# Out1's PSUM tiles regrouped from halves of the result to bank numbers, with other load times in the planner

## The chip, the cores and the metric

The kernel runs on one core of one Trainium2 chip. The time is device microseconds of one execution, compared as the median of several runs. TensorE (PE) has a queue of its own, as have VectorE (DVE), ScalarE (ACT), GpSimd (POOL) and SyncE (SP); each works off its queue in order, and engines wait for each other through semaphores. TensorE writes its results to PSUM (eight banks), and ScalarE and VectorE take them from there to SBUF.

## What is computed

The reference, cut to what matters (B = 8 batches, H = 8 heads, S = 576 tokens, D = 64, M = 32 memory slots; d_model 512, d_ff 2048):

```python
a = softmax(phi over S)                        # (B, H, S, M)
k_m, v_m = a^T k, a^T v                        # (B, H, M, D)
x = softmax(q k_m^T / 8) v_m                   # (B, H, S, D) -> (4608, 512)
h = x @ moe_w_in;  x = silu(h) @ moe_w_out     # first layer
h = x @ moe2_w_in; y = elu(h) @ moe2_w_out     # second layer
```

## The kernel before

**Arithmetic.** All is fp32. Large products are made of fp16 parts: an operand is split into a high and a low part, and a product is the sum of three matmuls (low x high, high x low, high x high; `mm3`). In the first layer the attention's output is not formed: `v_m` is multiplied into `w_in` first (`u_mm`, tile `u`), and the in1 product is attention weights `aT` times `u`.

**Stages.** A hand-written list does batch 0's attention and in1 and loads the first weights (to about 75 us). `plan_first` then plans the rest of batch 0's out1 and the batches 1 to 7: for each batch in1 (16 steps m, each 12 matmuls into one PSUM tile `ph`, followed by a silu on ScalarE) and out1 (below), beside which run the attention of a later batch (scores, softmax, transposes, `kvp`, `u`) and the conversion of the second layer's weights (`raw` to `quad` to `hl_q`, stored to `w2is` and `w2os` by POOL's queue). A second plan does the last batch's out1 and the whole second layer in nine token blocks (`h2A`, `h2D`, `o`).

**Out1 of a batch** (`plan_out1`) is a Strassen-like scheme: seven products j in the order 0, 1, 5, 6, 4, 3, 2 (p1, p2, p6, p7, p5, p4, p3 in the code). Each consists, for the two halves e = 0, 1 of the output features, of 8 units q; a unit is 3 matmuls of 128 x 288. The moving operands `T` are split from sums of `h` by ScalarE and VectorE. Products 0, 5, 4, 2 accumulate one after the other in bank 0, products 1, 6, 3 in bank 1 (`BANK`). After each product ScalarE copies (`copy_of`, line 177 `y<-ph`) or VectorE adds (`add_to`, line 1251 `y<-ph,io,y`) its bank to the result `y`, once for each half. POOL then stores a half of `y` to `x2d` (line 1280), and ScalarE squares it once that store has landed (line 353).

**PSUM.** Four banks are the pool `ps_m`, two tiles of two banks with one tag "m", handed out in turn. In in1 a tile holds one step m (two token halves). In out1 a tile holds one half e: its bank 0 and its bank 1.

**The planner** (`Plan`) takes tasks with an engine, a cost in us, a rank and dependences, simulates the engines, and emits the instructions in the simulated order. Products are main tasks with due times spread evenly over the plan; every other task is due ahead of what needs it by the costs between and, ahead of a product, by AHEAD. Weight conversions get due times between W2FROM and W2TO of the plan. Buffers are rings: a task that takes a slot depends on those that free it. Waits between engines are put in afterwards, from what instructions read and write; the planner's dependences are its own. A load costs 3.6 us + KB/350 in `plan_first` and depends on its ring's slot: `kv` has 3 slots and ten loads for each batch, q four.

Of the kernel before, what the change touches and what calls it, by code (L numbers as in the profile page):

```python
# [38 lines left out]
SA = 2.0 ** 14  # L39
NY = 2  # L40
NT = 3
NKV = 3
W2FROM, W2TO, AHEAD = 0.2, 0.92, 25
SHIFT = 9
WB_TAG = ("w0", "w1", "w2", "T2")
WR = ("w0", "w2", "w1")
# [43 lines left out]
def attn_moe_moe(ctx: ExitStack, tc: tile.TileContext, qT, phiT, kvm, kvt, w1i, w1o, w2i, w2o, out):  # L90
# [8 lines left out]
    dram = ctx.enter_context(tc.tile_pool(name="dram", bufs=1, space=bass.MemoryType.DRAM))  # L99
    ps_a = ctx.enter_context(tc.tile_pool(name="ps_a", bufs=4, space=PSUM))  # L100
    psum = ctx.enter_context(ExitStack())
    ps_m = psum.enter_context(tc.tile_pool(name="ps_m", bufs=2, space=PSUM))

    x2d = [dram.tile([P, KD, S], F32, name=f"x2d{b}") for b in range(B)]

# [81 lines left out]
    class Plan:  # L187
# [41 lines left out]
                        latest[d] = min(latest[d], latest[i] - self.tasks[d][1] - wait - (self.ahead if i in main else 0.0))  # L229
            self.tasks = [(t[0], t[1], latest[i], *t[3:]) for i, t in enumerate(self.tasks)]  # L230

        def load(self, kb, rank, fn, deps=()):

            return self.add("DMA", (2.2 if self.ahead is None else 3.6) + kb / 350, rank, fn, deps, kb / 350)

        def store(self, kb, rank, fn, deps=()):

# [646 lines left out]
    def plan_mem(pl, n, r, ex, ready):  # L884
# [21 lines left out]
        for g in range(NG):  # L906
            for c in range(NC):
                load, free = [], []
                if n > 1:
                    load = [pl.load(256, r - 300, lambda g=g, c=c: load_kv(n, g, c), pl.ring("kv", NKV))]  # L910
                    free = pl.take("kv", load[0])
                elif c == NC - 1:
                    free = pl.rings["kv"][1 + g][1]
                t = on("PE", 0.3, lambda g=g, c=c: mem_kv(n, g, c), load + es + (last or pl.ring(*C)))
                if not last:
                    kv_free = pl.take("c", t)
                last = [t]
                free.append(t)
            kv += last
# [43 lines left out]
    def plan_attn(pl, n, r, mem, after):  # L963


        A = "a", 2

        def on(eng, cost, fn, deps):
            return pl.add(eng, cost, r, fn, deps)

        qs, q_frees = [], []
        for p in range(NP):
            if n > 1:
                qs.append(pl.load(295, r - 290, lambda p=p: load_q(n, p), pl.ring("q", NP)))
# [55 lines left out]

    HALF = [slice(0, HS), slice(HS, S)]

    def ps_half():
        ps = ps_m.tile([P, 2, 512], F32, tag="m", name="ph")
        return ps[:, :, :HS], [ps[:, 0, :HS], ps[:, 1, :HS]]

    def y_tile(name="y"):
# [5 lines left out]

    def in1_first(m):
        z = st[0]
        pv, ps = ps_half()
# [6 lines left out]
    def plan_out1_first(pl, rank, ready):  # L1053
# [5 lines left out]

        def mm(d, q):  # L1060
            if q == 0:
                z[d] = ps_half()
            ks = range(4 * q, 4 * q + 4)
            for k in ks:
                for t in range(2):
# [6 lines left out]
        for d in range(KD):  # L1072
            for q in range(4):
                t = pl.product(4.25, rank + 4 * d + q, lambda d=d, q=q: mm(d, q),
                           last + ready[d] + (pl.ring("m", 2) if q == 0 else []))
                if q == 0:
                    free = pl.take("m", t)
# [9 lines left out]
    def plan_in1(pl, b, r, A, u, u_free, first, h_free):  # L1087
# [2 lines left out]
        z = st[b]  # L1090
        w = {}
        silus = []

        def mm(m):
            w[m], ps = ps_half()
            mm3(ps, HALF, [
                (z["u", g][:, 0, m * P:(m + 1) * P], z["u", g][:, 1, m * P:(m + 1) * P], z["aT"][:, 0, g], z["aT"][:, 1, g])
                for g in range(NG)
# [4 lines left out]
                out=h[m // KQ][:, :, m % KQ], in_=w.pop(m), func=AF.Silu, scale=z["inv1"][:, m // 4:m // 4 + 1])  # L1103

        for m in range(KF):
            t = pl.product(1.475, r + m, lambda m=m: mm(m), A["aT"] + [u[m // 4, g] for g in range(NG)] + pl.ring("m", 2))
            for free in u_free + [A["aT_free"]]:
                free.append(t)
            free = pl.take("m", t)
# [70 lines left out]
    def plan_out1(pl, b, r, silus, made, stored, scales, y_tile, y_ring):  # L1180

        z = st[b]
        w = [dict() for _ in range(2)]
        BANK = {0: (0, 0), 5: (0, 8), 4: (0, 16), 2: (0, 24), 1: (1, 0), 6: (1, 0), 3: (1, 8)}
        io = pl.add("DVE", 0.25, r - 2500, lambda: out_scale(b), scales + list(stored.values()))
        loads = {}

# [6 lines left out]

        def unit(e, j, q):
            bank, at = BANK[j]
            if "ps" not in w[e]:  # L1200
                w[e]["ps"] = ps_half()[1]
            t = z["T", WSEQ.index(j)]
            mm3([w[e]["ps"][bank]], [slice(0, HS)], [
                (w1s[b, j][:, e, 0, q], w1s[b, j][:, e, 1, q], t[:, 0, q], t[:, 1, q])
            ], at + q, at + KQ, skip_group_check=at > 0)

        last = {}
        free = {}
        took = {}
        count = [0]  # L1210

        def units(j, e, q, deps):
            bank = BANK[j][0]
            if e not in free:
                deps = deps + pl.ring("m", 2)
            t = pl.product(0.368, r + 0.5 * count[0], lambda: unit(e, j, q),
                       deps + [last.get((e, bank)), took.get(e), loads[j][0]] + z["made"].get((MOVING[j], q // 4), []))
            count[0] += 1
            if e not in free:
                free[e] = pl.take("m", t)  # L1220
                took[e] = t
            last[e, bank] = t
            loads[j][1].append(t)
            z["T_free", WSEQ.index(j)].append(t)
            return t

        def product(j, deps):

            t = [None, None]
            load(j)  # L1230
            if WSEQ.index(j) >= made:
                plan_moving(pl, b, WSEQ.index(j), r - 2400, silus)
            if j in (3, 2):
                for e in range(2):
                    for q in range(KQ):
                        t[e] = units(j, e, q, deps[e])
            else:
                for q in range(KQ):
                    for e in range(2):
                        t[e] = units(j, e, q, deps[e])  # L1240
            return t

        def copy_of(e, bank, s, deps):
            def fn():
                if "y" not in w[e]:
                    w[e]["y"] = y_tile()
                acopy(w[e]["y"][:, s], w[e]["ps"][bank], z["io1"][:, e:e + 1])
            return pl.add("ACT", act(HS), r - 2500, fn, deps)

        def add_to(e, bank, s, from_, deps):  # L1250
            return pl.add("DVE", dve(HS), r - 2500, lambda: nc.vector.scalar_tensor_tensor(
                out=w[e]["y"][:, s], in0=w[e]["ps"][bank], scalar=z["io1"][:, e:e + 1], in1=w[e]["y"][:, from_],
                op0=ALU.mult, op1=ALU.add), deps)

        E = range(2)
        C11, C12, C21, C22 = range(4)
        p1 = product(0, [[], []])
        yfree = []
        c1 = []
        for e in E:  # L1260
            c1.append(copy_of(e, 0, C11, [p1[e], io] + pl.ring(*y_ring)))
            yfree.append(pl.take(y_ring[0], c1[e]))
        p2 = product(1, [[], []])
        c11 = [add_to(e, 1, C11, C11, [c1[e], p2[e]]) for e in E]
        p6 = product(5, [[c] for c in c1])
        u2 = [copy_of(e, 0, C21, [p6[e], c1[e]]) for e in E]
        p7 = product(6, [[c] for c in c11])
        s7 = [copy_of(e, 1, C22, [p7[e], c1[e]]) for e in E]
        p5 = product(4, [[c] for c in u2])
        c22 = [add_to(e, 0, C22, C22, [p5[e], s7[e]]) for e in E]  # L1270
# [585 lines left out]
```

## Time and profile before

| | |
|---|---|
| median of 3 runs | 1422.68 us (1421.36 to 1424.61) |
| profiled execution, its own time | 1424.17 us |
| its span (first to last instruction) | 1422.4 us |
| busy: TensorE, VectorE, ScalarE, POOL | 1357.5, 1127.4, 952.3, 51.3 us |
| mean granted TensorE clock | 0.991 of full |

The span is what one profiled execution took from its first to its last instruction; the 1.8 us beside it lie around that. Busy time is the union of an engine's instructions. Idle time of an engine that is not the bottleneck costs nothing by itself. The ends of matmuls are modelled, and consecutive matmuls overlap in the listing. Line numbers are those of the code above; many matmuls have line 1019, that of the helper `mm3`, so they are told apart by their tiles: `ph<-aT,u` is in1, `ph<-T,w1s` out1.

### The profile page before, as it was taken

Reading aid. Unit: us, or ns where it says so; the run is one execution under the profiler, and the core shown is the slowest. Engines: PE = TensorE matmul, PEld = TensorE weight load, DVE = VectorE, ACT = ScalarE, POOL = GpSimd, SP = SyncE. Lnnn points to the kernel's source line nnn. Section 1 sums busy time; section 2 is a strip of 40 time slices with the busy share of each in tenths; the row PEclk is TensorE's granted clock in tenths of the full one; section 3 lists DMA queues with packets and bytes.
Section 4 is the critical chain, followed back from the end, with each engine's and each line's share of the span. In section 5 each row is a group of like instructions: output and inputs, shape, how many; then the busy total and the mean of one; then the engine's idle time right before and its main releaser. Section 6 shows DMA issues by size and latency. Waiting matters only on the chain.

```text
span 1422.4 us, 28662 instructions
## 1 busy us (share of the span) xinstructions
PE 1357.5 (95%) x12048; PEld 1092.2 (77%) x12048; DVE 1127.4 (79%) x1753; ACT 952.3 (67%) x1357; POOL 51.3 (4%) x85
## 2 busy tenths in 40 slices
PE   4998999999998999999998999999999999999998
PEld 3676667676766767676777888888888888888887
DVE  5878878788877988796767788787978787878794
ACT  3667765858756686675657576767767676857582
POOL 0001100010110010001000000000000000000000
PEclk8999999999999999999999999999999999999999
DMA  9465767467466475645195333242415151414130
GB/s 362 169 212 176 259 250 265 154 234 262 174 239 232 169 275 185 226 151 198 53 345 175 106 108 109 85 131 68 149 41 175 41 167 49 148 63 137 59 119 31
DMA packets 68801, 233.07 MB, mean 164 GB/s; under 512 B 9024, under 2 KB 15168, under 8 KB 64064
## 3 DMA queue, kind: packets, MB, share of 16 engines
q1 hardware_dynamic: 60288, 199.78, 41.6%
q0 software_dynamic: 8384, 31.46, 5.6%
q8 instruction: 94, 1.54, 0.5%
q14 instruction: 35, 0.29, 0.1%
HBM read 186.12 MB, written 40.89 MB: 160 GB/s over the span
## 4 chain that ended last, share of the span: by engine, by line
PE 73%; DMA 8%; DVE 7%; ACT 7%; issue 4%; SPq 0%; POOL 0%; ACTq 0%; POOLq 0%; DVEq 0%
PE ph L1019 24%; PE o L1019 20%; PE h2A L1019 11%; PE h2D L1019 8%; DMA wi<-w2is 3%; PE ph L1066 2%; PE up L859 2%; PE sc L774 2%; DMA kv<-in_kvm 2%; PE kvp L678 1%; PE ph L1026 1%; DMA w2is<-hl_q 1%; DVE h L133 1%; DMA raw<-in_w1o 1%; ACT y L177 1%
## 5 line engine op out<-in xcount | busy, mean ns | idle before, releaser
L1019 PE MATMUL o<-t,wq 128*128 128x256 f16 x3024 | 361.1, 273 | 1.8 <-DVE t L174 1.5
L1019 PEld LDWEIGHTS <-wi 128*128 128x128 f16 x3024 | 295.7, 98 | 49.2 <-issue 7.2
L1019 PEld LDWEIGHTS <-wq 128*128 128x128 f16 x3024 | 295.8, 98 | 37.0 <-issue 2.3
L1019 PE MATMUL ph<-T,w1s 128*128 128x288 f16 x2352 | 307.3, 286 | 12.3 <-ACT y L177 7.4
L1019 PEld LDWEIGHTS <-w1s 128*128 128x128 f16 x2352 | 226.2, 98 | 82.4 <-issue 26.2
L1019 PE MATMUL h2A<-xh,wi 128*128 128x256 f16 x1728 | 227.8, 273 | 9.3 <-ACT h L1460 5.2
L1460 ACT ACTIVATE h<-h2A,inv 128x256 f32<-128x256 f32 x288 | 133.2, 468 | 115.4 <-PE h2A L1019 112.1
L1019 PE MATMUL ph<-aT,u 128*128 128x288 f16 x1344 | 176.3, 286 | 1.3 <-ACT h L1102 1.0
L1019 PE MATMUL h2D<-xh,wi 128*128 128x256 f16 x1296 | 171.0, 274 | 0.1
L169 ACT ACTIVATE t<-h,s_g 128x768 f16<-128x768 f32 (+1 forms) x144 | 147.0, 1036 | 33.7 <-DVE h L1502 23.0
L174 DVE SCALAR_TENSOR_TENSOR t<-h,s_g,t 128x768 f16<-128x768 f32 (+1 forms) x144 | 162.9, 1144 | 5.7 <-ACT t L169 5.6
L1019 PEld LDWEIGHTS <-u 128*128 128x128 f16 x1344 | 127.0, 98 | 49.2 <-issue 18.9
L174 DVE SCALAR_TENSOR_TENSOR T<-h,c,T 128x1152 f16<-128x1152 f32 x98 | 137.0, 1411 | 19.5 <-ACT T L169 19.4
L1464 DVE SCALAR_TENSOR_TENSOR h<-h2D,inv,h 128x256 f32<-128x256 f32 x216 | 102.1, 479 | 60.7 <-PE h2D L1019 46.6
L169 ACT ACTIVATE T<-h,c 128x1152 f16<-128x1152 f32 x98 | 119.9, 1250 | 33.0 <-DVE h L133 22.2
L133 DVE TENSOR_TENSOR h<-h 128x256 f32<-128x256 f32 (+1 forms) x302 | 128.3, 462 | 3.0
L1502 DVE SCALAR_TENSOR_TENSOR h<-e,h 128x1024 f32<-128x1024 f32 x72 | 87.9, 1221 | 18.6 <-ACT e L1498 18.0
L1102 ACT ACTIVATE h<-ph,inv 128x576 f32<-128x576 f32 x112 | 81.7, 738 | 15.9 <-PE ph L1019 15.3
L1495 ACT ACTIVATE e<-h 128x1024 f32<-128x1024 f32 x72 | 75.5, 1049 | 14.1 <-DVE h L1464 13.8
L1498 ACT ACTIVATE e<-e 128x1024 f32<-128x1024 f32 x72 | 75.7, 1051 | 0.9
L1066 PE MATMUL ph<-h,w1o 128*128 128x288 f32 x256 | 66.1, 415 | 0.0
L133 DVE TENSOR_TENSOR h<-h,h 128x1152 f32<-128x1152 f32 x42 | 56.5, 1352 | 8.2 <-ACT h L1102 7.8
(183 smaller groups left out, 1279.2 us busy)
## 6 DMA issues: line engine op xcount, KB each, us to landing
w1s<-w1os SPq DMA_DIRECT2D x98, 512.0 KB, 4.6
wi<-w2is SPq DMA_DIRECT2D x56, 896.0 KB, 4.6
kv<-in_kvm SPq DMA_DIRECT2D x48, 256.0 KB, 5.1
q<-in_qT SPq DMA_DIRECT2D x32, 288.0 KB, 7.3
out<-ye SPq DMA_DIRECT2D x36, 256.0 KB, 2.0
raw<-in_w1i SPq DMA_DIRECT2D x8, 1024.0 KB, 11.3
raw<-in_w1o SPq DMA_DIRECT2D x8, 1024.0 KB, 4.9
raw<-in_w2i SPq DMA_DIRECT2D x8, 1024.0 KB, 6.9
```

The lines of the kernel that those rows point to most:

```text
L133: nc.vector.tensor_tensor(out=out, in0=a, in1=b, op=op)
L169: nc.scalar.activation(out=hi, in_=x, func=AF.Copy, scale=s)
L174: nc.vector.scalar_tensor_tensor(out=lo, in0=x, scalar=s, in1=hi, op0=ALU.mult, op1=ALU.subtract)
L774: nc.tensor.matmul(ps[o:o + 64, c // 2, 2 * p:2 * p + 2], z["q", p][:, t0:t0 + 64], z["kT"][:, p // 2, 64 * (p % 2):64 * (p % 2) + 64], st ...
L1019: nc.tensor.matmul(o, w, x[:, c], start=first, stop=last, **how)
L1066: nc.tensor.matmul(z[d][1][t], wB[d][:, k], h[k // KQ][:, t, k % KQ], start=(k == 0), stop=(k == KF - 1))
L1102: nc.scalar.activation(out=h[m // KQ][:, :, m % KQ], in_=w.pop(m), func=AF.Silu, scale=z["inv1"][:, m // 4:m // 4 + 1])
L1460: nc.scalar.activation(out=w["x"][:, s], in_=w["A"], func=AF.Copy, scale=inv)
L1464: return pl.add("DVE", COST["add"], base, lambda: nc.vector.scalar_tensor_tensor(out=w["x"][:, s], in0=w["D"], scalar=inv, in1=w["x"][:, s ...
L1495: nc.scalar.activation(out=w["e"], in_=w["x"][:, B21:], func=AF.Relu, scale=-1.0)
L1498: nc.scalar.activation(out=w["e"], in_=w["e"], func=AF.Exp, scale=-1.0)
L1502: nc.vector.scalar_tensor_tensor(out=x, in0=w["e"], scalar=-1.0, in1=x, op0=ALU.add, op1=ALU.max)
```

## The change

Out1's two PSUM tiles are taken by bank number: one tile holds bank 0 of both halves, the other bank 1 of both halves. The pool has two tags m0 and m1 with one tile each; in1's steps alternate between them, `mslot` keeps which is next. Units of all seven products now alternate between the halves, and every dependence on a product is one on both halves' last units. The copies that follow p3 free the one tile, the additions that follow p4 the other. In the planner, loads of `kv` are costed 1 us later (the 64-row tail 3 us, and at 128 KB), those of q 3 us later; W2TO goes from 0.92 to 0.95 and AHEAD from 25 to 35.

```diff
+KVLATE, QLATE = 1.0, 3.0
-W2FROM, W2TO, AHEAD = 0.2, 0.92, 25
+W2FROM, W2TO, AHEAD = 0.2, 0.95, 35
-    ps_m = psum.enter_context(tc.tile_pool(name="ps_m", bufs=2, space=PSUM))
+    ps_m = psum.enter_context(tc.tile_pool(name="ps_m", bufs=1, space=PSUM))
-        def load(self, kb, rank, fn, deps=()):
-            return self.add("DMA", (2.2 if self.ahead is None else 3.6) + kb / 350, rank, fn, deps, kb / 350)
+        def load(self, kb, rank, fn, deps=(), late=0.0):
+            return self.add("DMA", (2.2 if self.ahead is None else 3.6) + late + kb / 350, rank, fn, deps, kb / 350)
-                    load = [pl.load(256, r - 300, lambda g=g, c=c: load_kv(n, g, c), pl.ring("kv", NKV))]
+                    load = [pl.load(256 if c < NC - 1 else 128, r - 300, lambda g=g, c=c: load_kv(n, g, c), pl.ring("kv", NKV), KVLATE if c < NC - 1 else 3.0)]
-                qs.append(pl.load(295, r - 290, lambda p=p: load_q(n, p), pl.ring("q", NP)))
+                qs.append(pl.load(295, r - 290, lambda p=p: load_q(n, p), pl.ring("q", NP), QLATE))
-    def ps_half():
-        ps = ps_m.tile([P, 2, 512], F32, tag="m", name="ph")
+    mslot = [0]
+    def ps_half(k):
+        ps = ps_m.tile([P, 2, 512], F32, tag=f"m{k}", name="ph")
# plan_in1 (in1_first and plan_out1_first likewise)
+        at = mslot[0]
-            w[m], ps = ps_half()
+            w[m], ps = ps_half((at + m) % 2)
-            t = pl.product(1.475, r + m, lambda m=m: mm(m), A["aT"] + [u[m // 4, g] for g in range(NG)] + pl.ring("m", 2))
+            t = pl.product(1.475, r + m, lambda m=m: mm(m), A["aT"] + [u[m // 4, g] for g in range(NG)] + pl.ring(f"m{(at + m) % 2}", 1))
# plan_out1
+        SLOT = mslot[0], 1 - mslot[0]
+        mslot[0] = SLOT[1]
         def unit(e, j, q):
             bank, at = BANK[j]
-            if "ps" not in w[e]:
-                w[e]["ps"] = ps_half()[1]
+            if bank not in ps:
+                ps[bank] = ps_half(SLOT[bank])[1]
-            mm3([w[e]["ps"][bank]], [slice(0, HS)], [
+            mm3([ps[bank][e]], [slice(0, HS)], [
         def units(j, e, q, deps):
-            if e not in free:
-                deps = deps + pl.ring("m", 2)
+            if bank not in free:
+                deps = deps + pl.ring(f"m{SLOT[bank]}", 1)
         def product(j, deps):
-            if j in (3, 2):
-                for e in range(2):
-                    for q in range(KQ):
-                        t[e] = units(j, e, q, deps[e])
-            else:
-                for q in range(KQ):
-                    for e in range(2):
-                        t[e] = units(j, e, q, deps[e])
-            return t
+            return [units(j, e, q, deps) for q in range(KQ) for e in range(2)][-2:]
-        p6 = product(5, [[c] for c in c1])
-        u2 = [copy_of(e, 0, C21, [p6[e], c1[e]]) for e in E]
+        p6 = product(5, c1)
+        u2 = [copy_of(e, 0, C21, [c1[e]] + p6) for e in E]
...
-        c22 = [add_to(e, 0, C22, C22, [p5[e], s7[e]]) for e in E]
+        c22 = [add_to(e, 0, C22, C22, [s7[e]] + p5) for e in E]
-        p3 = product(2, [[c] for c in c22])
+        p3 = product(2, c22)
+        free[0] += c12
+        free[1] += c21
-            free[e] += [c11[e], c21[e], c12[e], c22[e]]
```

## Rows read from the trace of the kernel before

**Rows 1.** Summary: busy time by engine; the chain that ended last, by engine.
```profile
PE 1357.5 (95%) x12048; PEld 1092.2 (77%) x12048; DVE 1127.4 (79%) x1753; ACT 952.3 (67%) x1357; POOL 51.3 (4%) x85
...
PE 73%; DMA 8%; DVE 7%; ACT 7%; issue 4%; SPq 0%; POOL 0%; ACTq 0%; POOLq 0%; DVEq 0%
```

**Rows 2.** Windows: us; busy PE, PEld, DVE, ACT, POOL; clock, DMA share, GB/s.
```profile
160.00:735.00 575.00, 551.80 (x5113) 401.92 (x5112) 464.75 (x634) 392.14 (x558) 39.07 (x58) 1.00 0.61 214
650.00:700.00 50.00, 48.90 (x421) 34.63 (x419) 28.96 (x46) 28.96 (x41) 1.92 (x3) 1.00 0.29 98
752.00:756.00 4.00, 3.10 (x29) 2.64 (x27) 0.48 (x1) 0.67 (x2) 0.00 (x0) 1.00 0.91 370
756.00:764.00 8.00, 6.08 (x39) 4.68 (x39) 5.15 (x9) 7.75 (x13) 0.00 (x0) 0.79 0.37 118
800.00:1422.00 622.00, 610.71 (x5572) 543.97 (x5569) 491.04 (x826) 418.17 (x584) 0.37 (x1) 1.00 0.30 97
```

**Rows 3.** Waits of PE, 160 to 735: total us, times, longest.
```profile
PE ph L1019 <- ACT y L177: 7.4, 27, 0.9
PE kvp L678 <- DMA kv<-in_kvm: 6.4, 5, 2.2
PE ph L1019 <- DVE y L1251: 3.3, 9, 0.6
PE ph L1019 <- ACT h L1102: 2.4, 4, 0.9
PE aTp L826 <- DVE att L133: 1.1, 1, 1.1
PE kvp L678 <- ACT pad L177: 1.0, 1, 1.0
```

**Rows 4.** Timeline of PE: start, us, line, tiles, count, idle before.
```profile
272.88 1.63 PE L1019 MATMUL ph<-T,w1s 128*128 128x288 f16 x12
...
274.80 5.32 PE L1019 MATMUL ph<-T,w1s 128*128 128x288 f16 x42
280.34 0.53 PE L1019 MATMUL ph<-T,w1s 128*128 128x288 f16 x3 [0.22 <-ACT y L177]
```

**Rows 5.** Timeline of ACT in the same stretch.
```profile
279.78 0.89 ACT L177 ACTIVATE y<-ph,io 128x288 f32<-128x288 f32 x2 [1.27 <-PE ph L1019]
```

**Rows 6.** Timeline of PE: shortest and longest wait for a kv load.
```profile
348.86 0.43 PE L678 MATMUL kvp<-kv,es 128*32 128x128 f32 x8 [0.21 <-DMA kv<-in_kvm]
...
435.59 0.43 PE L678 MATMUL kvp<-kv,es 128*32 128x128 f32 x8 [2.17 <-DMA kv<-in_kvm]
```

**Rows 7.** DMA issues: count, KB each, median us to landing.
```profile
kv<-in_kvm SPq DMA_DIRECT2D x48, 256.0 KB, 5.1
```

**Rows 8.** Timeline: p4's end and the second addition after p5, batches 2 and 4.
```profile
308.72 5.69 PE L1019 MATMUL ph<-T,w1s 128*128 128x288 f16 x45
...
317.36 0.50 DVE L1251 SCALAR_TENSOR_TENSOR y<-ph,io,y 128x288 f32<-128x288 f32 x1
...
480.87 5.69 PE L1019 MATMUL ph<-T,w1s 128*128 128x288 f16 x45
...
490.39 0.50 DVE L1251 SCALAR_TENSOR_TENSOR y<-ph,io,y 128x288 f32<-128x288 f32 x1
```

**Rows 9.** Timeline of the last batch's handover to the second layer.
```profile
740.75 0.69 POOL L1280 DMA_DIRECT2D x2d<-y  x1 [39.25 <-ACT y L177]
746.32 0.68 POOL L1280 DMA_DIRECT2D x2d<-y  x1 [4.88 <-ACT h L1460]
...
755.81 1.16 ACT L353 ACTIVATE y<-y 128x1152 f32<-128x1152 f32 x1 [3.14 <-DMA x2d<-y]
...
757.48 0.81 PE L1019 MATMUL h2A<-xh,wi 128*128 128x256 f16 x6 [2.38 <-ACT h L1460]
```

**Rows 10.** Timeline: the last store of converted weights, the first load back.
```profile
658.88 0.55 POOL L443 DMA_DIRECT2D w2os<-hl_q  x1 [8.97 <-ACT u L169]
...
726.93 20.04 SPq L1321 DMA_DIRECT2D wq<-w2os  x14
```

More of the change, by code (lines that the diff above doesn't have):

```diff
@@ L1045, in in1_first @@
         z = st[0]
-        pv, ps = ps_half()
+        pv, ps = ps_half(m % 2)
         mm1(ps, HALF, [(z["u", g][:, m * P:(m + 1) * P], z["aT"][:, g]) for g in range(NG)])
@@ L1061, in mm @@
             if q == 0:
-                z[d] = ps_half()
+                z[d] = ps_half(d % 2)
             ks = range(4 * q, 4 * q + 4)
@@ L1074, in plan_out1_first @@
                 t = pl.product(4.25, rank + 4 * d + q, lambda d=d, q=q: mm(d, q),
-                           last + ready[d] + (pl.ring("m", 2) if q == 0 else []))
+                           last + ready[d] + (pl.ring(f"m{d % 2}", 1) if q == 0 else []))
                 if q == 0:
-                    free = pl.take("m", t)
+                    free = pl.take(f"m{d % 2}", t)
                 last = [t]
@@ L1105, in plan_in1 @@
         for m in range(KF):
-            t = pl.product(1.475, r + m, lambda m=m: mm(m), A["aT"] + [u[m // 4, g] for g in range(NG)] + pl.ring("m", 2))
+            t = pl.product(1.475, r + m, lambda m=m: mm(m), A["aT"] + [u[m // 4, g] for g in range(NG)] + pl.ring(f"m{(at + m) % 2}", 1))
             for free in u_free + [A["aT_free"]]:
                 free.append(t)
-            free = pl.take("m", t)
+            free = pl.take(f"m{(at + m) % 2}", t)
             silus.append(pl.add("ACT", act(S) - 0.02, r + m - 2000, lambda m=m: silu(m), [t, A["scales"]] + (silus[-1:] or first) + h_free(m)))
@@ L1186, in plan_out1 @@
         w = [dict() for _ in range(2)]
+        ps = {}
         BANK = {0: (0, 0), 5: (0, 8), 4: (0, 16), 2: (0, 24), 1: (1, 0), 6: (1, 0), 3: (1, 8)}
+        SLOT = mslot[0], 1 - mslot[0]
+        mslot[0] = SLOT[1]
         io = pl.add("DVE", 0.25, r - 2500, lambda: out_scale(b), scales + list(stored.values()))
@@ L1208, in plan_out1 @@
         free = {}
-        took = {}
         count = [0]
@@ L1213, in units @@
             bank = BANK[j][0]
-            if e not in free:
-                deps = deps + pl.ring("m", 2)
+            if bank not in free:
+                deps = deps + pl.ring(f"m{SLOT[bank]}", 1)
             t = pl.product(0.368, r + 0.5 * count[0], lambda: unit(e, j, q),
-                       deps + [last.get((e, bank)), took.get(e), loads[j][0]] + z["made"].get((MOVING[j], q // 4), []))
+                       deps + [last.get(bank), loads[j][0]] + z["made"].get((MOVING[j], q // 4), []))
             count[0] += 1
[L1219 to L1222, printed above, removed]
+            if bank not in free:
+                free[bank] = pl.take(f"m{SLOT[bank]}", t)
+            last[bank] = t
             loads[j][1].append(t)
@@ L1227, in product @@
         def product(j, deps):
-            t = [None, None]
             load(j)
@@ L1246, in fn @@
                     w[e]["y"] = y_tile()
-                acopy(w[e]["y"][:, s], w[e]["ps"][bank], z["io1"][:, e:e + 1])
+                acopy(w[e]["y"][:, s], ps[bank][e], z["io1"][:, e:e + 1])
             return pl.add("ACT", act(HS), r - 2500, fn, deps)
@@ L1251, in add_to @@
             return pl.add("DVE", dve(HS), r - 2500, lambda: nc.vector.scalar_tensor_tensor(
-                out=w[e]["y"][:, s], in0=w[e]["ps"][bank], scalar=z["io1"][:, e:e + 1], in1=w[e]["y"][:, from_],
+                out=w[e]["y"][:, s], in0=ps[bank][e], scalar=z["io1"][:, e:e + 1], in1=w[e]["y"][:, from_],
                 op0=ALU.mult, op1=ALU.add), deps)
@@ L1256, in plan_out1 @@
         C11, C12, C21, C22 = range(4)
-        p1 = product(0, [[], []])
+        p1 = product(0, [])
         yfree = []
@@ L1260, in plan_out1 @@
         for e in E:
-            c1.append(copy_of(e, 0, C11, [p1[e], io] + pl.ring(*y_ring)))
+            c1.append(copy_of(e, 0, C11, p1 + [io] + pl.ring(*y_ring)))
             yfree.append(pl.take(y_ring[0], c1[e]))
-        p2 = product(1, [[], []])
-        c11 = [add_to(e, 1, C11, C11, [c1[e], p2[e]]) for e in E]
-        p6 = product(5, [[c] for c in c1])
-        u2 = [copy_of(e, 0, C21, [p6[e], c1[e]]) for e in E]
-        p7 = product(6, [[c] for c in c11])
-        s7 = [copy_of(e, 1, C22, [p7[e], c1[e]]) for e in E]
-        p5 = product(4, [[c] for c in u2])
-        c22 = [add_to(e, 0, C22, C22, [p5[e], s7[e]]) for e in E]
-        p4 = product(3, [[c] for c in s7])
-        c21 = [add_to(e, 1, C21, C21, [p4[e], u2[e]]) for e in E]
-        p3 = product(2, [[c] for c in c22])
-        c12 = [copy_of(e, 0, C12, [p3[e], c1[e]]) for e in E]
+        p2 = product(1, [])
+        c11 = [add_to(e, 1, C11, C11, [c1[e]] + p2) for e in E]
+        p6 = product(5, c1)
+        u2 = [copy_of(e, 0, C21, [c1[e]] + p6) for e in E]
+        p7 = product(6, c11)
+        s7 = [copy_of(e, 1, C22, [c1[e]] + p7) for e in E]
+        p5 = product(4, u2)
+        c22 = [add_to(e, 0, C22, C22, [s7[e]] + p5) for e in E]
+        p4 = product(3, s7)
+        c21 = [add_to(e, 1, C21, C21, [u2[e]] + p4) for e in E]
+        p3 = product(2, c22)
+        c12 = [copy_of(e, 0, C12, [c1[e]] + p3) for e in E]
+        free[0] += c12
+        free[1] += c21
         done = []
         for e in E:
-            free[e] += [c11[e], c21[e], c12[e], c22[e]]
             def store(e=e):
```

## The prediction

> **What bounds the kernel now.** I read the profile's summary first: TensorE is busy for 95% of the span and holds 73% of the chain that ended last [rows 1]. Then the stages. From 160 to 735 us, where batches 1 to 7 run (attention, in1, out1), TensorE is busy 551.8 of 575.0 us, VectorE 464.8, ScalarE 392.1, at a granted clock of 1.00; from 800 us on, the last layer has 610.7 of 622.0 us [rows 2]. So TensorE is the bound, 23.2 us of idling lie in the first of these stages, and the diff plans only that stage anew, with the handover behind it. Third, the list of what TensorE waited for in that stage [rows 3]: ScalarE's `y` 7.4 us in 27 waits, the loads of `kv` 6.4 in 5, VectorE's `y` 3.3 in 9, ScalarE's `h` 2.4 in 4, and 2.1 for two steps of the attention chain.
>
> What the 36 waits on `y` are is seen in the timeline. In the second batch the matmuls of out1 (`ph<-T,w1s`) begin at 272.88; up to 280.34 there are 12 + 42 = 54 of them [rows 4]. A unit is 3 matmuls and a product 16 units, so the one that waits at 280.34 is unit 2 of the second product (p2). Nothing that p2 computes with comes from `y`: it writes bank 1. What it waits for is ScalarE's copy of bank 0 at 279.78, and that copy had itself waited 1.27 us for TensorE [rows 5]. The two banks belong to one tile (`ps_half` with tag "m", one tile for each half e), and the wait goes by tile: TensorE writes e's bank 1 only after ScalarE has read e's bank 0, and the copy starts only after the units already put into that tile. This is a handshake that the arithmetic doesn't need, and the planner doesn't know it.
>
> **The change part by part.** The sum is made for the profiled execution, 1424.2 us (span 1422.4 and 1.8 around it), 1.5 above the median of 1422.7; the total goes onto the median.
>
> (a) *Banks by product.* The new tile holds one bank number for both halves. The copies or additions behind product k read one tile while product k+1 writes the other one. The 36 waits lose their cause. One costs more than its printed idle time, because a matmul's end lies behind the start of the next: 42 matmuls take 5.32 us and 3 take 0.53 [rows 4], so the pitch is (5.32 - 0.53) / 39 = 0.123 and a matmul by itself 0.53 - 2 x 0.123 = 0.284. A stop therefore costs its gap plus 0.16 us. That makes 7.4 + 3.3 + 36 x 0.16 = **16.5 us**. No instruction goes or comes; only the order of units within p3 and p4 changes (halves alternate now), at the same count. Bounds: 0, if the wait isn't by tile, and 16.5.
>
> Would the stops have cost clock as well? The granted clock over the whole stage is 1.00 [rows 2], so I add nothing. (The Trainium skill, page "TensorE: Matmul & The Clock Gate", section "A second HAM failure mode: psum-queue depth-cycling", says that short idles between groups of matmuls, as PSUM banks are cycled, can make the clock fall back again and again. By that rule the gain would be larger than the gaps; by the row it is not.)
>
> (b) *Loads planned later.* The planner takes 3.6 us + KB/350 for a load: 4.3 for `kv`, 4.4 for q. It now takes 5.3 for `kv`, 7.0 for the tail, 7.4 for q. The median measured for the `kv` loads is 5.1 [rows 7], so the model comes to fit. Their matmuls move back in TensorE's queue by 1 us or more. The five waits range from 0.21 to 2.17 us [rows 6]; 1.0 less on four and 0.2 on one is **4.2 us**. Bounds 0 (the load lands later too: its own slot is freed by these matmuls) and 6.4 + 5 x 0.16 = 7.2. No wait on q is in the list, so q's 3 us buy nothing, and cost nothing while the attention chain has room.
>
> (c) *First product of out1.* It now needs only the tile of in1's step 14, not those of 14 and 15. Waits on `h` are 2.4 us in four [rows 3]; I take **1.0**, bounds 0 and 2.4 + 4 x 0.16 = 3.0.
>
> (d) *AHEAD 35.* All that feeds a product, attention included, is due 10 us earlier. The two waits of that chain, 2.1 us [rows 3]: I take **1.0**, bounds 0 and 2.4.
>
> (e) *A new wait.* p3, the last product, reuses the tile of p5, so its first unit now waits for both additions `c22` (VectorE, 0.5 us each); before, half 1 of p3 came eight units later and only it needed the second one. In batches 2 and 4 the second addition after p5 ended at 317.86 and 490.89, when p4 had ended at 314.41 and 486.56 [rows 8]: 3.5 and 4.3 us late, as VectorE was working on attention. Behind TensorE's wait stand all of p3 and in1. The new need gives the second addition an earlier due time, which moves it ahead of some of that work, so I charge a third of these two rows, **+2.5**, bounds 0 and 3.5 + 4.3 = 7.8; were all seven batches as late as the worst, 30. The next in1 starts on the tile that p4 leaves and needs p3's tile only 1.5 us later, and two copies of 0.45 us fit there: 0.
>
> (f) *The handover at 735 to 765.* The two stores of `y` to `x2d` left at 740.75 and 746.32, ScalarE stood 3.14 us in its queue until the second had landed (its squares began at 755.81), behind it stood a copy of `h`, and TensorE stood 2.38 us [rows 9]; then the clock was 0.79 from 756 to 764 [rows 2]. Now both halves end together, the first store loses its 5.6 us of lead, and the second shares its way with it: 576 KB at the 370 GB/s of that stretch [rows 2] is 1.6 us more. With some clock I take **+2**; bounds +5.6 (the whole lead) and -4.1 (the stop and 8 x 0.21 = 1.7 of clock both gone).
>
> (g) *W2TO 0.95.* The last conversions of the second layer's weights move back by 0.03 of a stage of 575 us [rows 2], about 17 us. The last store of them on POOL's queue is at 658.88 and would be at 676, still ahead of the first load that reads them back on SP's queue, at 726.93 [rows 10]. Their VectorE work moves into a stretch where that engine is busy 29.0 of 50 us [rows 2]. Cost 0; the margin of 68 us would have to go three times over 17 before a reader waits.
>
> Sum: -16.5 - 4.2 - 1.0 - 1.0 + 2.5 + 2.0 = **-18.2 us**. VectorE's load in the stage rises from 464.8/575 = 81% to 464.8/556 = 84%, below TensorE's. 1422.7 - 18.2 = **1404.5 us**.
>
> **Rivals.** *Given back.* The false waits go, but p3 waits at 7.8, the handover loses 5.6, and `kv` gains nothing: -16.5 - 1 - 1 + 7.8 + 5.6 = -5.1, 1417.6 us. For it: VectorE's lateness [rows 8] and one engine queue behind one store [rows 9]. Against: the planner sees p3's need as a true dependence and can put other matmuls there; the false wait it couldn't see.
>
> *Slower.* VectorE's additions `c22` at p3: TensorE waits for them in each of the seven batches as long as the worst row says, 4.3 us. That is 30 instead of 2.5: -18.2 + 27.8 = +9.6, 1432.3 us. It decides from 20.7 / 7 = 3.0 us in each batch. For it: two rows show such lateness. Against: they came with a due time that allowed it.
>
> *The change doesn't do it.* The wait on `y` isn't by tile but, for example, by the whole PSUM pool, so the stops stay: -1.7, 1421.0 us, not to be told from no change (I call 0.2%, 2.8 us, what a measurement here can tell). Against: the copy and the stopped unit fall on one tile exactly [rows 4, 5].
>
> *Everything fits.* All waits for loads, `h` and attention go too (7.2, 3.0, 2.4), p3 costs nothing, and the handover gains 4.1: 16.5 + 7.2 + 3.0 + 2.4 + 4.1 = 33.2, 1389.5 us. Against: a new order of so many tasks leaves some late ones.
>
> **How the numbers follow.** The forecast, 1398 to 1412 by itself, has 0.68; given back 0.12; everything fits 0.08; slower 0.07; no effect 0.05. The range 1394 to 1417 leaves out the last two and parts of two others. Faster by over 0.2%: 0.68 + 0.12 + 0.08 = 0.88; within 0.2%: 0.05; slower: 0.07.
>
> **What would show it.** (a) no wait of `ph` for `y` in p2 to p5, and ScalarE's own wait for `ph` (a copy following its product) shorter than the 1.27 us; out1 without stops of 0.22. (b) waits on `kv` under 3 us in total. (e) any wait of p3's first unit on VectorE's `y`. (f) the two `x2d` stores within 1.5 us of each other, and TensorE's stop behind ScalarE at the handover. From 800 us on the stage must be as long as before. I am wrong if waits on `y` remain in number, or if VectorE shows up as what TensorE waits for.

## The result and the profile after

The changed kernel takes 1409.26 us (median of 4 runs, 1405.95 to 1411.22) against 1422.80 us for the kernel before: a ratio of 0.9902 [0.9877, 0.9927], 13.9 us faster [10.4, 17.5]. The forecast was 1404.5 us in a range of 1394 to 1417. The profiled execution took 1407.48 us with a span of 1405.5; against the span of before, 1422.4, that is 16.9 us less, and the accounts below are made in it.

The summary of the kernel after: TensorE's busy time is nearly that of [rows 1], in a span 16.9 us shorter; in the chain that ended last its share is 79% instead of 73%, those of VectorE and ScalarE 4% each instead of 7%. The last row is the group of out1's matmuls (count, busy us, mean ns, idle before them): no idle time at all.

```profile
PE 1354.2 (96%) x12048; PEld 1092.9 (78%) x12048; DVE 1127.9 (80%) x1753; ACT 951.1 (68%) x1357; POOL 51.1 (4%) x85
...
PE 79%; DMA 7%; DVE 4%; issue 4%; ACT 4%; POOL 0%; SPq 0%; ACTq 0%; POOLq 0%; DVEq 0%
...
L1020 PE MATMUL ph<-T,w1s 128*128 128x288 f16 x2352 | 301.9, 286 | 0.0
```

What TensorE waited for from 160 to 735 us, to be laid beside [rows 3] (total us, times, longest):

```profile
PE ph L1020 <- ACT h L1106: 8.5, 6, 4.3
PE kvp L679 <- DMA kv<-in_kvm: 1.9, 2, 1.3
PE up L860 <- DVE u L175: 1.0, 2, 0.8
PE h2A L1020 <- ACT h L1457: 0.9, 2, 0.5
```

Both rows on `y` are gone (10.7 us in 36 waits), the waits on `kv` have fallen from 6.4 to 1.9, but those on ScalarE's `h` have risen from 2.4 in four to 8.5 in six, one of them 4.3 us long.

The windows of the same kernel (us; busy PE, PEld, DVE, ACT, POOL; clock, DMA share, GB/s) show what became of the clock, which stood at 1.00 in the whole stage before [rows 2]:

```profile
160.00:735.00 575.00, 562.33 (x5198) 415.26 (x5197) 468.76 (x643) 397.88 (x570) 39.49 (x58) 0.99 0.62 220
333.00:338.00 5.00, 4.93 (x32) 3.18 (x31) 4.35 (x6) 4.40 (x8) 0.00 (x0) 0.66 0.44 146
415.00:423.00 8.00, 5.60 (x31) 3.15 (x31) 5.19 (x5) 5.81 (x7) 1.68 (x3) 0.57 0.52 181
740.00:760.00 20.00, 14.58 (x100) 11.36 (x100) 14.63 (x26) 15.74 (x23) 0.00 (x0) 0.83 0.27 94
800.00:1390.00 590.00, 586.17 (x5353) 522.51 (x5351) 475.41 (x802) 410.34 (x573) 0.37 (x1) 1.00 0.31 100
```

Three short stretches were at the lower level of 1.2 GHz for a part of their time: 5 x 0.34 / 0.5 = 3.4 us in the first, 8 x 0.43 / 0.5 = 6.9 in the second, 20 x 0.17 / 0.5 = 6.8 at the handover, there in two parts, from 743.4 and from 753.7 us on. Where they lie is seen in TensorE's timeline (start, us, line, tiles, count, idle before): out1 now runs 69 matmuls in one piece across a change of bank (first row), and the stops are in in1 of batches 3 and 4 and at the handover.

```profile
202.92 8.63 PE L1020 MATMUL ph<-T,w1s 128*128 128x288 f16 x69
...
333.07 4.77 PE L1020 MATMUL ph<-aT,u 128*128 128x288 f16 x24 [2.02 <-ACT h L1106]
...
342.86 1.63 PE L1020 MATMUL ph<-aT,u 128*128 128x288 f16 x12 [0.97 <-ACT h L1106]
...
409.23 3.30 PE L1020 MATMUL ph<-aT,u 128*128 128x288 f16 x24
...
417.40 3.04 PE L1020 MATMUL ph<-aT,u 128*128 128x288 f16 x12 [4.27 <-ACT h L1106]
...
743.41 1.44 PE L1020 MATMUL h2A<-xh,wi 128*128 128x256 f16 x6 [3.88 <-ACT h L1457]
```

The same 24 matmuls take 3.30 us at 409.23 and 4.77 behind the stop at 333.07; 12 take 1.63 at 342.86 and 3.04 at 417.40. Each long stop is paid for a second time.

Why ScalarE's `h` comes late stands in ScalarE's own timeline of the same kernel:

```profile
331.27 1.12 ACT L311 ACTIVATE quad<-raw 128x1024 f32<-128x1024 f32 x1 [3.11 <-DMA raw<-in_w2i]
332.28 0.74 ACT L1106 ACTIVATE h<-ph,inv 128x576 f32<-128x576 f32 x1
...
341.05 1.13 ACT L311 ACTIVATE quad<-raw 128x1024 f32<-128x1024 f32 x1 [2.43 <-DMA raw<-in_w2i]
342.09 0.72 ACT L1106 ACTIVATE h<-ph,inv 128x576 f32<-128x576 f32 x1
...
415.57 1.15 ACT L170 ACTIVATE hl_q<-quad,s_w2i 128x1024 f16<-128x1024 f32 x1 [4.23 <-DMA w2is<-hl_q]
416.63 1.35 ACT L1106 ACTIVATE h<-ph,inv 128x576 f32<-128x576 f32 x2
...
738.75 1.16 ACT L354 ACTIVATE y<-y 128x1152 f32<-128x1152 f32 x1 [3.00 <-DMA x2d<-y]
```

In front of each late silu (`h<-ph,inv`), and of the copies of `h` behind 741.38 at the handover, stands an instruction that TensorE's next matmuls don't need and that waits for a transfer: a conversion of the second layer's weights that waits for its load (`raw`), one that waits until a store has freed its buffer (`w2is`), and at the handover the squares that wait for `x2d`. ScalarE takes its queue in order, so `h` waits with it, and TensorE waits for `h`.

What the transfers themselves do is seen in POOL's queue (the next stores) and in the chain of waits between 310 and 350 us of the same kernel (start, us, what; `issue` stands where the profile shows nothing that was waited for):

```profile
317.64 0.72 POOL L448 DMA_DIRECT2D w2is<-hl_q  x1 [4.73 <-DVE u L175]
318.44 0.67 POOL L1277 DMA_DIRECT2D x2d<-y  x1
325.18 0.68 POOL L1277 DMA_DIRECT2D x2d<-y  x1 [6.08 <-issue]
...
407.31 0.78 POOL L1277 DMA_DIRECT2D x2d<-y  x1
415.78 0.68 POOL L1277 DMA_DIRECT2D x2d<-y  x1 [7.69 <-issue]
...
729.45 1.43 POOL L1277 DMA_DIRECT2D x2d<-y  x2 [41.01 <-ACT y L178]
```

```profile
317.64 7.22 DMA w2is<-hl_q
...
325.05 6.19 DMA raw<-in_w2i
...
336.17 4.86 DMA raw<-in_w2i
```

The two halves of `y` are finished together, so at 318 us a store of `w2is` (512 KB) and two of `x2d` (576 KB) come at once. The first lands 7.22 us after its issue; the load of `raw`, whose buffer it frees, leaves 0.19 us behind its landing and takes 6.19 us. The planner has 4.0 + 512/200 = 6.6 us for such a store and 4.0 + 590/200 = 7.0 for one of `x2d`. From issue to landing the trace gives 7.2, 8.4, 9.1 and 9.0 us for the four stores issued between 317.6 and 327.1, and 3.3 us for each of the three `w2is` stores issued between 422.7 and 430.0, when no other store of POOL's queue was under way and no load was issued. So beside other transfers these four land 0.6 to 2.4 us later than planned, and a load or a conversion that waits for a buffer takes the delay over. It need not be an `x2d` store that slows them: the `w2is` store of 433.55 took 9.1 us beside a load of `raw` issued at 433.36, with no other store of POOL's queue under way.

Late transfers are not new, however. The issues by kind (count, KB each, median us to landing), first of the kernel before, then of the kernel after:

```profile
raw<-in_w2i SPq DMA_DIRECT2D x8, 1024.0 KB, 6.9
x2d<-y POOLq DMA_DIRECT2D x14, 576.0 KB, 7.4
w2is<-hl_q POOLq DMA_DIRECT2D x14, 512.0 KB, 5.1
```

```profile
raw<-in_w2i SPq DMA_DIRECT2D x8, 1024.0 KB, 6.7
x2d<-y POOLq DMA_DIRECT2D x14, 576.0 KB, 8.8
w2is<-hl_q POOLq DMA_DIRECT2D x14, 512.0 KB, 5.2
```

Only the `x2d` stores got slower, by 1.4 us. The transfers that in1 of batches 3 and 4 stands for, `raw` and `w2is`, take by the median what they took before, when single `w2is` stores at the same places took 6.9 and 8.8 us (317.73 and 411.31). What changed is the place in ScalarE's queue, and in time, at which an instruction meets such a transfer.

### The profile page after: what moved, and what is told of

Its sections match the earlier page's. It is cut to its first block, busy times and chain, and to the rows that moved or that the text cites. A ratio compares the mean times of both kernels' runs of the same rounds, so it can differ in the third digit from the quotient of the medians.

```text
span 1405.5 us, 28627 instructions
## 1 busy us (share of the span) xinstructions
PE 1354.2 (96%) x12048; PEld 1092.9 (78%) x12048; DVE 1127.9 (80%) x1753; ACT 951.1 (68%) x1357; POOL 51.1 (4%) x85
## 4 chain that ended last, share of the span: by engine, by line
PE 79%; DMA 7%; DVE 4%; issue 4%; ACT 4%; POOL 0%; SPq 0%; ACTq 0%; POOLq 0%; DVEq 0%
PE ph L1020 24%; PE o L1020 22%; PE h2A L1020 12%; PE h2D L1020 9%; PE ph L1069 4%; DMA wi<-w2is 3%; PE ph L1027 2%; PE sc L775 2%; PE up L860 2%; PE kvp L679 1%; DMA kv<-in_kvm 1%; DMA x2d<-y 1%; DMA raw<-in_w2i 1%; DMA w2is<-hl_q 1%; DVE T L175 1%
## 5 line engine op out<-in xcount | busy, mean ns | idle before, releaser
L1020 PE MATMUL ph<-T,w1s 128*128 128x288 f16 x2352 | 301.9, 286 | 0.0
L1020 PE MATMUL ph<-aT,u 128*128 128x288 f16 x1344 | 179.8, 290 | 8.8 <-ACT h L1106 8.5
```

The source lines that it names most:

```text
L1020: nc.tensor.matmul(o, w, x[:, c], start=first, stop=last, **how)
```

## The experiments

Theory, as it stood before the runs: the grouping by bank brings what the false waits cost and leaves out1's arithmetic alone; what the whole change falls short by is lost because the new planner's numbers and the new, common end of both halves put `x2d` stores, conversion stores and loads beside each other, and ScalarE's queue stands for transfers that land later than the planner costs them. Rivals: the tiles' grouping itself brings the late `h` (in1 alternates between two single tiles); POOL's queue alone is what delays the stores; a new order of the plan scatters by some us anyhow.

### 1. Banks alone

The new tiles with the old planner's numbers.

```diff
-KVLATE, QLATE = 1.0, 3.0
-W2FROM, W2TO, AHEAD = 0.2, 0.95, 35
+KVLATE, QLATE = 0.0, 0.0
+W2FROM, W2TO, AHEAD = 0.2, 0.92, 25
-                    load = [pl.load(256 if c < NC - 1 else 128, ..., KVLATE if c < NC - 1 else 3.0)]
+                    load = [pl.load(256, r - 300, lambda g=g, c=c: load_kv(n, g, c), pl.ring("kv", NKV))]
```

> The banks by product as in the changed kernel; AHEAD 25, W2TO 0.92 and the load costs as before. Both theories: no wait of out1's matmuls on y (36 before). Theory T (the pairing itself crowds POOL's store queue: both x2d stores leave together, conversion stores wait behind them, ScalarE waits for those and the silus come late): waits of ph on ACT h over 5 us in all, as in the changed kernel, a stretch at half clock between 200 and 700 us, 1408 to 1413 us. Rival R (the planner's new numbers moved conversion steps into in1, where they block ScalarE): waits on ACT h at most 3 us, no such stretch, 1404 to 1407 us, that is 1422.8 less 16.5.

Measured: 1402.51 us, ratio 0.9874 [0.9846, 0.9902], so 18.0 us faster, more than the whole change by the medians (their intervals overlap). From 160 to 735 us, TensorE's waits for `h` and `kv` and then ScalarE's for `x2d`:

```profile
PE ph L1020 <- ACT h L1106: 4.3, 3, 3.4
PE kvp L679 <- DMA kv<-in_kvm: 1.3, 2, 0.9
```

```profile
ACT y L354 <- DMA x2d<-y: 8.2, 2, 5.0
```

The timeline of ScalarE has the longer of the two:

```profile
420.81 1.16 ACT L354 ACTIVATE y<-y 128x1152 f32<-128x1152 f32 x1 [5.03 <-DMA x2d<-y]
```

No wait on `y` is left. Here too one late `h` appears in batch 4, with 6.8 us at the lower clock behind it, but behind the squares of `y` and not behind the conversions. So the new tiles bring a wait on `x2d` of their own, and the planner's numbers decide which of ScalarE's instructions meets a late transfer. The time is below what either theory expected; the 4.3 us on `h` lie between the two, and the stretch at the lower clock is theory T's. The waits on `kv` are down to 1.3 us, and 0.9 on its tail, without the later costs of these loads.

### 2. The planner's numbers alone

The kernel before with KVLATE, QLATE, W2TO and AHEAD as in the change; the tiles stay by half.

> The tiles by half as before; AHEAD 35, W2TO 0.95 and the later loads of kv and q as in the changed kernel. Both theories: the waits on y stay, 30 to 40 of them and over 9 us; waits on kv under 3 us in all. T: waits on ACT h at most 3 us, 1417 to 1421 us (before less the kv waits). R: waits on ACT h over 6 us with a stretch at half clock, 1422 us or more.

Measured: 1417.12 us, 0.9976 [0.9959, 0.9994], 3.4 us faster. TensorE's waits from 160 to 735 us:

```profile
PE ph L1020 <- ACT y L178: 7.3, 29, 0.8
PE ph L1020 <- DVE y L1252: 4.4, 11, 0.6
...
PE kvp L679 <- DMA kv<-in_kvm: 2.1, 4, 1.0
PE ph L1020 <- ACT h L1103: 1.3, 3, 0.7
```

`kv` falls from 6.4 to 2.1 us as in the whole change, the false waits stay, in1 of batches 3 and 4 takes 29.8 and 30.7 us (34.4 and 36.0 in the whole change, 30.2 and 32.6 before), and no stretch of the stage is at the lower clock. The numbers by themselves don't make `h` late. 18.0 and 3.4 would add to 21.4; the change has 13.9. The two together lose 7.5 us; as each of the three gains has an interval of 2.5 to 4 us to either side, this is known to some 6 us only.

### 3. The stores of x2d on SP's queue

```diff
-                nc.gpsimd.dma_start(out=x2d[b][:, e::2], in_=...)
+                nc.sync.dma_start(out=x2d[b][:, e::2], in_=...)
```

> The changed kernel, with out1's stores of y to x2d issued by SP's queue instead of POOL's (the planner still costs them as before). T: ScalarE's wait of 4.2 us for the w2is store goes, waits of ph on ACT h fall from 8.5 us to under 4, no half clock between 200 and 700 us, 1400 to 1405 us. R: the waits on ACT h stay over 6 us and the time within 3 us of the changed kernel's 1409.

Measured: 1408.02 us, 0.991 [0.989, 0.9931], as the change. `h` is waited for 8.1 us in six, in1 of batches 3 and 4 takes 34.4 and 34.0 us, ScalarE still stands 4.8 us for `raw` and 3.1 for `w2is`. At the handover its wait for `x2d` fell to 0.7 us, but TensorE then stood 3.2 us for the weights `wi`. The expectation that this recovers the loss failed: that `x2d` stores share POOL's queue isn't the cause. The conversion stores still leave that queue 0.3 us behind the landing of the one before (at 326.93, 416.68 and 421.39), so this run doesn't show what their waiting for each other costs.

### 4. Banks and load times, AHEAD and W2TO as before

```diff
-W2FROM, W2TO, AHEAD = 0.2, 0.95, 35
+W2FROM, W2TO, AHEAD = 0.2, 0.92, 25
```

> The changed kernel with AHEAD 25 and W2TO 0.92 as before; banks by product and later loads of kv and q kept. T: as the changed kernel within 3 us, 1406 to 1412, waits on ACT h over 5 us. R, with AHEAD and W2TO as what moves conversions: waits on ACT h at most 3 us, kv waits under 3 us, 1401 to 1405 us.

Measured: 1406.95 us, 0.9901 [0.9881, 0.9922]; `h` 7.9 us in five, in1 of batch 4 37.2 us and of batch 3 29.8; ScalarE stands 4.5 us for `raw` of `w2o` and 3.7 for `w2is`. So the waits on `h` come with the later costs of `kv` and q alone; with AHEAD and W2TO as in the change they fall into another batch. By the medians this is 4.4 us above experiment 1, but the two intervals overlap.

### 5 and 6. Squares of y planned later, in experiment 1 and in the change

The planner is told that a store of `x2d` lands 7 us later, so the squares move back in ScalarE's queue; the second layer's first PSUM tiles, which the plan opened behind all of the last out1's tasks, no longer wait in it for the squares.

```diff
-        def store(self, kb, rank, fn, deps=()):
+        def store(self, kb, rank, fn, deps=(), late=0.0):
-            return self.add("POOL", 4.0 + kb / 200, rank, fn, deps, 1.2)
+            return self.add("POOL", 4.0 + late + kb / 200, rank, fn, deps, 1.2)
-            t = pl.store(590, r - 2500, store, [c11[e], c12[e], c21[e], c22[e]])
+            t = pl.store(590, r - 2500, store, [c11[e], c12[e], c21[e], c22[e]], 7.0)
-        pl.gates[1] = [pl.add("PE", 0.0, 0, open_ps_o, out1)]
+        pl.gates[1] = [pl.add("PE", 0.0, 0, open_ps_o, out1[1:4] + out1[5:])]
```

> As e1_banks_only, but the planner costs out1's x2d stores 7 us longer (so the squares behind them stand later in ScalarE's queue), and the second layer's PSUM tiles no longer wait for the squares in the plan. Theory (ScalarE's in-order queue stands for stores that land later than the planner costs, since both halves now leave together): ScalarE's wait for x2d, 9.6 us in e1_banks_only, under 1; in1 of batch 4 from 35.4 us to 32 or less; TensorE's stop at the handover from 4.0 us to under 1.5; 1391 to 1396 us. Rival (ScalarE has too much work there, the wait only shows where): the stops stay within 1 us of what they were, 1400 us or more.

> The changed kernel with the same two edits (x2d stores costed 7 us longer, no squares ahead of the second layer's PSUM tiles). Theory: the handover gains as in e6, but in batches 3 and 4 ScalarE waits for the converted weights' transfers (raw, w2is) and not for x2d, so in1 of batches 3 and 4 stays at 33 us or more and a half-clock stretch remains between 300 and 430; 1401 to 1406 us. Rival: no gain, 1407 us or more.

Measured: 1403.79 us, 0.9869 [0.985, 0.9888], on experiment 1, and 1407.44 us, 0.9898 [0.9878, 0.9918], on the change; neither differs from what it was built on. Both times are above what was expected (1391 to 1396 and 1401 to 1406). In both ScalarE's wait for `x2d` is gone, and at the handover TensorE's longest stop on `h` fell from 4.0 to 0.6 us in the first, where its longest is now 1.4 us, for `wi`. But from 160 to 735 us 4.2 us on `kv`, 2.0 on its tail and 2.2 on the attention took its place in the first, with 10.2 us at the lower clock behind the stops on `kv` and its tail, and in1 of batch 4 takes 35.4 us as in experiment 1; in the second `raw` (5.6 us) and `w2is` (4.5) stay, in1 of batches 3 and 4 at 34.6 and 34.0 us. One late transfer of three isn't enough.

### 7 and 8. The conversions' transfers planned later as well

On experiments 6 and 5: loads of the second layer's weights and stores of the converted ones cost 3 us more in the plan.

```diff
-            t = pl.store(512, rank, lambda i=i, j=j: store(e, j, z["hl"][:, i]), [r])
+            t = pl.store(512, rank, lambda i=i, j=j: store(e, j, z["hl"][:, i]), [r], 3.0)
-            load = pl.load(1024, 0, lambda k=k: load64(src, e, k), pl.ring("raw", 2))
+            load = pl.load(1024, 0, lambda k=k: load64(src, e, k), pl.ring("raw", 2), 3.0)
```

> e7 with the planner also costing the raw loads of the second layer's weights and the stores of converted weights 3 us longer. Theory: ScalarE's waits for raw and w2is (9.7 us in the changed kernel) fall under 3, in1 of batches 3 and 4 takes 32 us or less, no half clock between 200 and 700 us, 1392 to 1398 us. Rival (AHEAD 35 and W2TO 0.95 put too much work into in1): in1 of batches 3 and 4 stays at 33 us or more, 1401 us or more.

> e6 with the planner also costing the raw loads and the stores of converted weights 3 us longer; AHEAD 25, W2TO 0.92, loads of kv and q as before. Theory: within 3 us of e6 or better, 1389 to 1396 us, no half clock between 200 and 700 us. Rival: 1400 us or more.

Measured: on the change **1395.02 us, 0.9810 [0.9792, 0.9828]**, 26 us faster than the kernel before and the fastest of all; on the banks alone 1398.70 us, 0.9833 [0.9816, 0.985], above the 1396 expected at most. Of the first of the two, from 160 to 735 us TensorE's waits, ScalarE's for these transfers, and the windows:

```profile
PE ph L1020 <- ACT h L1106: 2.6, 5, 1.1
PE kvp L679 <- DMA kv<-in_kvm: 2.1, 3, 0.9
```

```profile
ACT hl_q L170 <- DMA w2is<-hl_q: 2.0, 1, 2.0
ACT quad L311 <- DMA raw<-in_w2i: 0.3, 1, 0.3
```

```profile
160.00:735.00 575.00, 565.99 (x5286) 420.13 (x5284) 476.61 (x655) 406.73 (x583) 41.70 (x60) 1.00 0.64 227
...
740.00:760.00 20.00, 18.21 (x161) 15.46 (x159) 16.71 (x30) 16.94 (x27) 0.00 (x0) 1.00 0.40 127
```

The waits on `h` are back at 2.6 us, in1 of batches 3 and 4 takes 30.1 and 30.7 us, the clock is 1.00 in the stage and at the handover. The transfers are no faster: the four stores of `x2d` of batches 2 and 3 land 9.1, 9.6, 8.6 and 5.7 us after their issue. What waits for them only stands further back in ScalarE's queue.

### 9 and 10. Each of the two costs alone

Experiment 6 with only the loads, and with only the stores, 3 us later.

> e7 with only the raw loads of the second layer's weights costed 3 us longer. If the loads are what ScalarE stands for in batch 3 (raw 5.6 us): in1 of batch 3 at 31 us or less, but the wait for w2is (4.5 us) and the long in1 of batch 4 stay; 1400 to 1404 us. If the loads are late only because the stores of converted weights free their buffers late: in1 of batch 3 stays at 33 us or more, 1405 us or more.

> e7 with only the stores of converted weights costed 3 us longer. If these stores are the root (they free the buffers that the raw loads and the next parts take): waits for raw and w2is both under 3 us, in1 of batches 3 and 4 at 32 us or less, 1394 to 1399 us. If not: only the w2is wait goes, in1 of batch 3 stays at 33 us or more, 1400 us or more.

Measured: 1410.15 us, 0.991 [0.9887, 0.9933], and 1407.26 us, 0.9887 [0.9865, 0.9908], so that neither expected gain came. TensorE's waits with the loads alone later:

```profile
PE kvp L679 <- DMA kv<-in_kvm: 10.2, 4, 4.1
PE ph L1020 <- ACT h L1106: 4.9, 7, 1.7
```

The wait for `raw` went and 10.2 us on `kv` came: these loads stand in SP's queue, also in order, behind `raw` loads that wait for a buffer (one of them stood 17.7 us for a `w2is` store); that this is what held `kv` up was read from the order of the queue and not tried. With the stores alone later, `raw` still cost 3.7 us of ScalarE and `kv` 6.5 of TensorE. The gain of 12 us between experiments 6 and 7 needs both.

### 11. The best planner's numbers with tiles by half

Experiment 7 with all of its planner's numbers, but the tiles and the order of units as in the kernel before.

> e8 with the PSUM tiles by half as before the change: all of e8's planner numbers, none of its banks. Theory (the wait by tile costs TensorE 0.38 us at each of some 36 places, whatever else is planned): 30 to 40 waits on y, and 14 to 19 us over e8's 1395, that is 1409 to 1414 us. Rival (the numbers of the planner alone bring the gain): 1395 to 1402 us.

Measured: 1417.59 us, 0.9975 [0.9959, 0.9991]. TensorE's waits, and the window of the stage:

```profile
PE ph L1020 <- ACT y L178: 9.5, 32, 1.0
PE ph L1020 <- DVE y L1252: 4.7, 10, 0.6
```

```profile
160.00:735.00 575.00, 550.14 (x5088) 400.69 (x5081) 464.09 (x634) 392.32 (x558) 41.10 (x58) 1.00 0.60 214
```

With the same numbers the grouping is worth (0.9975 - 0.9810) x 1422 = 23 us, by the intervals about 20 to 27, above the 14 to 19 expected. Of these, 9.5 + 4.7 + 42 x 0.16 = 20.9 us are the false waits, by the price that the prediction gave each.

### 12. Loads of q as before

Experiment 7 with QLATE = 0.

> e8 with the loads of q costed as before (3 us less). As the prediction had it (no wait on q, so these 3 us buy nothing): 1395 us within 2.8. Rival (q's later time also moves the attention chain out of the way): 1399 us or more, with waits of sc on the loads of q.

Measured: 1398.35 us, 0.9828 [0.981, 0.9847]; no wait on q appears. Beside the 0.9810 of experiment 7 the intervals overlap, so it isn't told apart whether q's 3 us do anything.

## Why the prediction was right, and where it failed

*(a) Right.* The 36 waits on `y` are gone, as in every run with tiles by bank, and they are there (40 and 42) in both runs with tiles by half (2, 11). 16.5 us was the predicted price; the comparison at equal numbers gave 23, of which 20.9 are these waits. Banks alone gave 18.0, but that run also lost waits on `kv` and gained some on `h`. That the wait went by tile is shown; the rival "doesn't do it" is out. With 42 such stops in the stage the granted clock was 1.00 (experiment 11). The rule of the Trainium skill that the prediction weighed here (page "TensorE: Matmul & The Clock Gate", section "A second HAM failure mode: psum-queue depth-cycling"), that repeated small idles lower the clock, did not hold for these stops. At the handover of the changed kernel, though, short stops were followed by a lower clock: behind three of 0.53, 0.77 and 0.70 us, the last of them just ahead of 753.78, it was at 1.2 GHz from 753.7 to 757.1 us.

*(b) Right in size, the cause not shown.* `kv` fell from 6.4 us in five waits to 1.9 in two, 4.5 + 3 x 0.16 = 5.0 us where 4.2 was said; the numbers alone gave 3.4 us in all. But banks alone, with the loads costed as before, brought these waits to 1.3 us as well. Over the kernels of this study they are 0 to 10.2 us with the later costs (experiments 4 and 9) and 1.3 to 6.4 us without, so any new order of the plan moves them.

*(d) Right in size, the cause not shown.* The two waits of 2.1 us are gone and 1.0 us on `u` came, a gain of 1.1 for the 1.0 forecast. With AHEAD at 25 (experiment 1) the waits on the attention chain are 1.1 us as well.

*(e) Wrong in size, to the good.* 2.5 us were charged for p3's wait on both additions. Out1's matmuls have no idle time before them at all; the rival "slower" had no ground.

*(f) About right.* Both stores left together at 729.45, ScalarE's queue stood for the squares, and TensorE stopped 3.88 us, then ran for 3.4 us at the lower clock, as it did again at 753.7. Up to the 336th matmul of the second layer's output the handover cost about 2.5 us more than before (2.0 forecast), but from the last product of out1 to the end it is 678.7 us against 678.4, so nearly all was made up again and 0.3 is left of the 2.0.

*(g) Right.* The last store of converted weights left at 663.22 us, and the first load that reads them back at 710.50, so a margin of 47 us is left.

*(c) The step that failed.* The prediction said that waits on ScalarE's `h` would fall by 1.0 us because p1 needs one tile only. They rose from 2.4 to 8.5 us, and with 3.4 and 5.2 us of work at half the clock behind the stops (4.3 us lost) this term is +10.7 instead of -1.0. The mechanism was in the prediction, but only at the handover, in (f): ScalarE's queue standing for a transfer later than planned. In (c) the wait on `h` was taken for a matter of PSUM tiles, when it is one of what stands ahead of the silu in ScalarE's queue. Experiments 2, 7, 9 and 10 show it: without the new tiles there is no such stop; with the conversions' transfers costed later the stops go and 12 us come back; with one of the two costs the wait only moves. The rival "everything fits" (1389.5 us) came within 5.5 us of what experiment 7 reached once the planner knew these times. The rival that in1's single tiles bring the late `h` falls with experiment 7 too, which has the same tiles. Mere scatter is not out as to the size: with tiles by bank, kernels that differ in the planner's numbers took 1395 to 1410 us. For the costs speaks that the same edit gained twice (12 us from experiment 6 to 7, and 5 us from 5 to 8, where the intervals just touch) and that the waits on `raw` and `w2is` fell with it.

In the profiled execution the stage from in1 of batch 1 to the end of out1 of batch 7 shrank by 15.0 us. The terms are -16.5 (y), -5.0 (kv), +6.4 (`h` with the 0.16 of two more stops), -1.1 (attention) and +4.3 (clock): -11.9. The other 3.1 us aren't put down to a row. 2.2 us more lie ahead of the stage, where the instructions up to the first matmul of out1 are the same and this matmul came between 73.2 and 77.5 us in the kernels of this study (76.2 before, 74.7 after). So the forecast of -18.2 was 1.3 us from the profiled execution and 4.3 us from the medians, and its total is right by luck. (c) missed 11.7 us; (e), charged too high, gave back 2.5, (f) 1.7, (b) 0.8, (d) 0.1, and 5.3 came from the 3.1 without a row and the 2.2 ahead of the stage, which no term of the prediction names.

What stays open: how much of the stores' lateness is the sharing of the DMA engines and how much a limit on stores in flight in POOL's queue. Stores often left 0.3 us after an older one had landed, with two in flight (325.18 and 415.78) and with one (426.32 and 429.95), but at 170.55 a third store left while two were under way. Experiment 3 doesn't separate the two. Why the planner put these conversions ahead of the silus in the changed kernel and not in experiment 2, which costs the transfers the same, was not followed through the planner.

## What to carry to other kernels

A tile is the unit in which waits are made: banks that are written and read in turn belong into tiles of their own, and a copy that waits for a neighbour's product is the sign. When a plan orders in-order queues, look on every engine for the instruction *ahead* of the late one, and cost transfers by what they take beside the others at that place (here up to 9.6 us for 3.3 in a quiet stretch), all links of a chain at once; correcting one link moved the wait to the next here. A gain at one place changes which instruction stands behind which transfer, so after the change the planner's costs are to be read again from its own trace.

## What the runs showed of the hardware

- 42 stops on `y` of up to 1.0 us in a stage left the granted clock at 1.00 (experiment 11), and so did a single stop of 2.17 us in the kernel before [rows 6]. In the changed kernel a stop of 2.02 us was followed by 3.4 us at the 1.2 GHz level, one of 4.27 us by the same level until 422.6 us, the stop of 3.88 us at the handover by 3.4 us, and three stops of 0.53, 0.77 and 0.70 us close behind each other by 3.4 us.
- A 512 KB store took 3.3 us from issue to landing with no load issued and no other store under way, up to 9.0 us beside two of 576 KB, and 9.1 us beside a load of 1 MB.
- Stores of `w2is` left POOL's queue 0.3 us after the one before them had landed, and with two stores in flight a third left 0.31 us after a landing, with up to 7.69 us in which POOL did nothing; three stores of `w1os` were in flight together at 170.55.
